# Query, key and value weights loaded one row chunk at a time, and an opening that multiplies the queries chunk by chunk

## The chip, the core and the metric

The kernel runs on one core of one Trainium2 chip. Times are device microseconds of that core. PE is the matmul engine (PEld its weight loads), DVE, ACT and POOL the vector, scalar and GpSimd engines, SP the engine whose queue issues nearly all DMAs.

## The reference, cut to what matters

A layer norm, an attention that carries 8 memory rows from one segment of 32 tokens to the next, a residual sum, and an MLP with its own layer norm. All in bfloat16.

```python
def _A_ref(x, mem0, Wq, Wk, Wv, Wo, seg_len):      # x: 1 x 2048 x 512, H = 32 heads of 128
    ...
    for s in range(n_seg):                          # 64 segments, one after the other
        xs = x[:, s * seg_len:(s + 1) * seg_len, :].copy()
        h = jnp.concatenate([mem, xs], axis=1)      # 8 memory rows + 32 tokens
        q = jnp.einsum('btd,dhe->bhte', h, Wq)
        k = jnp.einsum('btd,dhe->bhte', h, Wk)
        v = jnp.einsum('btd,dhe->bhte', h, Wv)
        scores = jnp.einsum('bhqe,bhke->bhqk', q, k) * scale
        ...
        o = jnp.einsum('bhqk,bhke->bhqe', p, v)
        o = jnp.einsum('bhte,hed->btd', o, Wo)
        mem = o[:, :M, :].copy()                    # what the next segment waits for
        outs.append(o[:, M:, :])
h = x + _A_ref(_layernorm(x, axis=-1), A_mem0, A_Wq, A_Wk, A_Wv, A_Wo, A_seg_len)
h2 = h + _B_ref(_layernorm(h, axis=-1), B_w1, B_b1, B_w2, B_b2)   # gelu(y w1 + b1) w2 + b2, F = 1792
```

Each of Wq, Wk, Wv is 512 x 4096, 4 MB; so is Wo. The 512 rows (`d`) lie on 128 partitions in four chunks of 128 rows (`DC = 4`).

## The kernel before

All weights stay in SBUF: `WQ`, `WK`, `WV` as `[128, 4 chunks, 4096]`, `WO` as `[128, 32, 512]`. A projection of a segment is a pass: for each of the four chunks four matmuls (one for each group of 32 output partitions, side by side on PE), summed in one PSUM bank. A pass gives one half `r` of the 4096 columns. Chunk `c` of half `r` of a weight is a key such as `("WQ", r, c)`; a matmul waits for the DMA that wrote its key.

The 32 tokens of a segment are split. Tokens 0 to 23 with the 8 memory rows are pack A (`hT`); the last 8 tokens of four segments together are pack B (`hB`), a block. `V0`, `K0`, `Q0` and so on are passes of pack A; `("B", "Q", b, (r, bank))` is the pass of pack B of block `b` for the queries' half `r` into a PSUM bank. `SC0`, `SC1` are the scores of each half, `PV0`, `PV1` the products with the values, `SA` the scores of rows without the last 8 tokens, `WO` the output projection in eight units, of which unit `q` reads two pieces of WO.

A recorder (`Sched`) takes every instruction with what it reads and writes; PE's order is written out by hand, and a planner orders the other engines by due times and puts the waits in. For segment 0 the hand-written order is the tuple `START`: strings are parts, `("T", "WO", a, b)` places units `a` to `b - 1` of the projection, `("W", bank, n)` places `n` fill matmuls of 128x512 that nobody reads (function `warm`). A query pass is evacuated by ACT (line 895) or DVE, transposed by DVE in 32x32 blocks (line 917) and copied into `ZC` (lines 931 and 938) for the scores.

SP issues, in this order: four DMAs of 1 MB for each of WV, WK and WQ (line 779), 16 of 256 KB for WO (line 796), then rows of x. The first two tiles of x (`xr`) and two small inputs go through ACT's queue. DVE takes the statistics of both x tiles, then normalizes them; PE's projections start behind that.

Segments 1 to 63 follow `ORDERS`. The memory rows of segment `s` leave as DVE's transpose of the projection (`TT`, line 1191) and a sum into `hT` (line 1185), for which segment `s + 1` waits. `fold` puts the projection of pack B into `opT` on POOL, in pieces of seven instructions; `nat` transposes `opT` back by DMA, adds x, stores `h_mid` and takes the second norm's statistics (`rs2`, on POOL).

The MLP runs in four blocks of 512 rows. Block 0's first matrix product (`w1_first`) is mixed into the end of the attention: six of its 14 column groups are kept as sums and activated later (`gelu_kept`), eight go through PSUM banks 5 and 6 in turn (`early`). `p2_load` fetches rows of `h_mid`, `p2_res` adds the bias row to them on POOL (`hb`, line 1323), the second product (line 1601) sums into four `quad` banks, and DVE adds `hb` to each of these (line 1655) before the next block may write the bank.

Of the kernel before, what the change touches and what calls it, by code (L numbers as in the profile page):

```python
# [104 lines left out]
STEP = 10.28  # L105
OPEN_BANK = dict(K0=4, K1=5, Q0=6, Q1=7, V0=5, V1=4, SC0=6, SC1=7, SA=5, WO=4)
START = (("B", "V", 0, (0, 6), (1, 7)), "V", "X", "S", ("B", "V", 1, (0, 6), (1, 7)), ("B", "K", 0, (0, 4), (1, 6)), "K0", "K1", ("B", "K", 1, (0, 4), (1, 6)),
         ("B", "Q", 0, (0, 5)), "Q0", ("B", "Q", 0, (1, 4)), "Q1", "Z", "SC0", "SC1", ("B", "Q", 1, (0, 5)), "PV0", "PV1", "SA", "WO", ("T", "WO", 0, 3),
         ("T", "WO", 3, 5), ("B", "Q", 1, (1, 6)), ("T", "WO", 5, 6), ("W", 7, 4), ("T", "WO", 6, 7), ("W", 7, 4), ("T", "WO", 7, 8))


def planned(o):
# [456 lines left out]
D = 512  # L569
DC = 4  # L570
# [6 lines left out]
NS = NTOK // SEG  # L577
NTB = NTOK // P
# [48 lines left out]
def build_kernel(nc, A_x, A_mem0, A_Wq, A_Wk, A_Wv, A_Wo, B_w1, B_b1, B_w2, B_b2, out):  # L627
    scale = float(E) ** -0.5
    S = Sched(nc)
    st = contextlib.ExitStack()  # L630
    with st:
# [35 lines left out]
        EC = sb("EC", [P, 2, 2, 64], F32)  # L667
# [3 lines left out]
        SA = sb("SA", [P, 8, 32], F32)  # L671
# [100 lines left out]
        def load(fn, kb, writes):  # L772
            chain.append(S.dma(fn, kb, writes=writes))
        chain, spread = [], {}

        def load_w(W, wd, key):
            for r in range(2):
                for c0 in (0, 2):
                    load(lambda e, r=r, c0=c0: e.dma_start(W[:, c0:c0 + 2, r * 2048:(r + 1) * 2048], wd[:, c0:c0 + 2, r * 2048:(r + 1) * 2048]),  # L779
                         1024, [(key, r, c0), (key, r, c0 + 1)])  # L780

        def first(fn, kb, writes):
            S.dma(fn, kb, writes=writes, eng="act")
# [57 lines left out]
        def warm(bank, n):  # L841

            def f(e):
                for _ in range(n):
                    ins = e.matmul(ps[bank][:, :], ident[:], WV[:, 0, 0:512], start=True, stop=True)
# [474 lines left out]
        def p2_res(k):  # L1320

            for t in range(TBS):
                S.op("pool", lambda e, t=t: e.tensor_tensor(hb[:, k % 2, t, :], hx_of(k)[:, t, :], b2bc[:], ALU.add), reads=[("hx", k % 2), "b2bc"],
                     writes=[("hb", k % 2, t)], after=used["WV"] + S.users([("rs2", NTB - 1)]), dur=1.1)
# [30 lines left out]
        def hx_early(t, after):  # L1355
            S.dma(lambda e: e.dma_start(xT_row, hd[:, t, :]), 128, reads=[("hd", t)], writes=["xT"], after=after)
            S.op("dve", lambda e: e.tensor_scalar(xn[:, t % 2, :], xT_row, agg2[:, t, 0:1], rst2[:, t:t + 1], ALU.subtract, ALU.mult),
                 reads=["xT", ("ag2", t), ("rs2", t)], writes=[("hn0", t), ("xn", t % 2)], dur=0.4)

        def hn_early(t, after):  # L1360
            S.dma(lambda e: e.dma_start_transpose(hnT0[:, :, t, :], xn[:, t % 2, :]), 256, reads=[("xn", t % 2)], writes=[("hnT", "first", t), ("xr", 2 + t)], after=after)

        def gelu_kept(fc):
            g = gT0_home[fc // 2][0][:, fc % 2, :]
            S.op("act", lambda e: e.activation(g, g, ACTF.Gelu_apprx_tanh, bias=b1t[:, fc:fc + 1], scale=1.0),
                 reads=[("gT0", fc), "b1t"], writes=[("gT0", fc)] + gT0_home[fc // 2][1], dur=0.65 + 1.3 * (fc == 0), after=[S.last_writer["SA"], S.last_writer[("EC", 1)]])
# [36 lines left out]
        for s in range(NS):  # L1403
# [48 lines left out]
            def tail(s):  # L1452
                S.tag = (s, "SAT")
                sa_tail(s)
                n = 14 if s == NS - 1 else (4, 4, 6, 0)[s % 4] if s // 4 < NTB - 3 else (7, 7, 0, 0)[s % 4]
                moved = []
                for f in late[::-1]:
                    moved.append(f([S.last_writer[("PTC", 1)]] + [o_ for o_ in moved if o_]))
                late[:] = now
                now.clear()  # L1460
                behind = [S.last_writer[(k, 1)] for k in ("PC", "PCa")] + [o_ for o_ in moved if o_]
                if folds:
                    fold(n, behind + [S.last_writer[("BD", s % 2, j)] for j in range(4 * (s == NS - 1))])
                if turned and s % 4 == 3:
                    for f in turned:
                        f(behind)
                    turned.clear()
                if 0 < s < NS - 1:
                    qb_fill(s + 1, [S.last_writer[("KA", s % 2, 0)]])
                S.tag = None  # L1470
# [55 lines left out]
                    wo(s, bank_of[name], mem=(s + 1 < NS), xrows=(s > 1))  # L1526
            if s == 0:

                for n in START:
                    if n[0] == "B":  # L1530
                        _, what, b, *halves = n
                        for r, bank in halves:
                            if what == "V":
                                v_B(b, r, bank)
                            else:
                                kq_B(b, "KQ".index(what), r, bank)
                    elif n[0] == "T":
                        S.take((0, n[1]), n[2], n[3])
                    elif n == "WO":
                        S.tag = (0, n)  # L1540
                        part(n)
                        S.tag = None
                    elif n[0] == "W":
                        warm(n[1], n[2])
                    elif n == "X":
                        ln1(1)
                    elif n == "S":
                        v_B_turn()
                    elif n == "Z":
# [63 lines left out]
        for i in range(2):  # L1613
            f = slice(i * (F // 2), (i + 1) * (F // 2))
            for c in range(DC):
                S.dma(lambda e, f=f, c=c: e.dma_start(W1[:, c, f], w1_d[:, c, f]), 224, writes=[("W1", i, c)], after=used["WK"])
        p2_load(0)
        p2_norm(1)
        p2_T(1)

# [4 lines left out]
                9: lambda: wo(NS + 1, later[0], mem=False), 11: lambda: nat(NTB - 1)}  # L1625
        rest = dict(zip((0, 1, 2, 3, 4, 5, 7), rest.values()))
        for n, fc in enumerate(range(6, FC)):
            w1_first(fc, early[fc % 2])
            rest.get(n, lambda: None)()
            if n < 6:  # L1630
                gelu_kept(n)
        p2_res(0)
        for fc in range(FC - 4):
            p2_w2(0, fc)
# [79 lines left out]
```

## Time and profile before

| | us |
|---|---|
| median of 3 runs (801.57 to 803.1) | 802.11 |
| the profiled execution | 802.59 |
| its span, from first to last instruction | 800.9 |
| PE busy in the span | 772.0 (96%) |
| DVE, ACT, POOL busy | 616.2, 545.7, 350.9 |

A row of a timeline has its start and length in us, engine, line, operation, `out<-in`, shapes and count, and in brackets how long the engine had been idle and what ended that. A row of the chain of waits has start, length and what the end of the execution hung on at that time. A row of a DMA has how long the issue kept the queue, and below it the time from issue to landing. Ends of matmuls are modelled: a group of N columns side by side shows some 0.2 us more than the step to the next group.

### The profile page before, as it was taken

How to read it: one execution, taken by the hardware profiler on the slowest of the kernel's cores; microseconds unless marked ns; L12 is line 12 of the kernel's file. 1: busy time of each engine (PE TensorE's matmuls, PEld its weight loads, DVE VectorE, ACT ScalarE, POOL GpSimd, SP SyncE). 2: the span in 40 equal slices, each digit the busy share in tenths (PEclk: the TensorE clock that was granted, in tenths of full speed). 3: DMA queues.
4: the chain of work that ended last, by engine and by line, in shares of the span. 5: the costliest groups of instructions: out<-in, count | busy, mean ns of one | idle time of the engine just before them, and what ended most of it. 6: DMA issues, size and time to landing. Idle time of an engine off the chain costs nothing.

```text
span 800.9 us, 43680 instructions
## 1 busy us (share of the span) xinstructions
PE 772.0 (96%) x19403; PEld 417.2 (52%) x18737; DVE 616.2 (77%) x1975; ACT 545.7 (68%) x1622; POOL 350.9 (44%) x886
## 2 busy tenths in 40 slices
PE   3788999999999999999999999999999999999998
PEld 1345555555555555555555555555555555544444
DVE  3267898898989898998989898989898888834211
ACT  1456777777777777777777777777777777743342
POOL 5023334545454545454545454545563535367200
PEclk9999999999999999999999999999999999999999
DMA  8960010110101010101020102020202131275200
GB/s 340 392 191 16 5 27 14 29 32 23 36 18 43 18 43 11 50 7 47 10 51 10 50 10 52 10 51 3 51 23 69 36 80 40 74 169 147 70 27 26
DMA packets 65594, 48.04 MB, mean 60 GB/s; under 512 B 29044, under 2 KB 61820, under 8 KB 65404
## 3 DMA queue, kind: packets, MB, share of 16 engines
q1 hardware_dynamic: 65072, 44.98, 19.3%
q8 instruction: 150, 2.46, 1.3%
q14 instruction: 40, 0.33, 0.1%
q10 hardware_dynamic: 332, 0.27, 0.1%
HBM read 31.08 MB, written 8.13 MB: 49 GB/s over the span
## 4 chain that ended last, share of the span: by engine, by line
PE 90%; DMA 3%; DVE 2%; SPq 2%; POOL 1%; ACT 1%; issue 0%; POOLq 0%
PE ps L876 44%; PE ps L1179 15%; PE ps L609 7%; PE quad L1601 5%; PE ps L1586 4%; PE ps L1218 4%; PE quad L1083 3%; DMA WQ<-in_A_Wq_dram 2%; SPq L779 2%; PE ps L1113 2%; PE quad L1045 2%; PE quad L1151 2%; PE quad L1088 1%; PE ps L1378 1%; PE ps L1375 1%; DMA oN<-opT 1%
## 5 line engine op out<-in xcount | busy, mean ns | idle before, releaser
L876 PE MATMUL ps<-WQ,hT 128*32 128x512 bf16 x2048 | 156.4, 382 | 3.5 <-DVE hT L1185 3.3
L1179 PE MATMUL ps<-WO,OT 128*32 128x256 bf16 x4224 | 140.6, 275 | 0.5 <-ACT OT L894 0.5
L876 PE MATMUL ps<-WV,hT 128*32 128x512 bf16 x1780 | 138.4, 380 | 0.0
L895 ACT ACTIVATE kq<-ps 128x512 bf16<-128x512 f32 x146 | 87.2, 597 | 55.9 <-PE ps L876 55.6
L1134 POOL TENSOR_TENSOR PA<-SA,rsa 128x256 bf16<-128x256 f32 x64 | 39.8, 622 | 184.2 <-DVE rsa L1127 172.3
L894 ACT CAST kq<-ps 128x512 bf16<-128x512 f32 x162 | 94.5, 583 | 29.1 <-PE ps L876 28.3
L1179 PEld LDWEIGHTS ps<-WO,OT 128*32 128x32 bf16 x4224 | 96.3, 97 | 22.1 <-issue 1.7
L1140 POOL COPY BD<-PTA 32x192 bf16<-32x192 bf16 x256 | 96.0, 375 | 16.2 <-DVE PTA L1136 0.4
L1070 DVE SCALAR_TENSOR_TENSOR PC<-EC,rsc,even 128x128 bf16<-128x128 f32 x256 | 94.5, 370 | 6.7
L876 PE MATMUL ps<-WK,hT 128*32 128x512 bf16 x1292 | 91.9, 379 | 0.0
L876 PEld LDWEIGHTS ps<-WQ,hT 128*32 128x32 bf16 x2048 | 55.2, 96 | 68.6 <-issue 20.1
L917 DVE STREAM_TRANSPOSE KALL<-kq 128x256 f32<-128x256 f32 x160 | 70.5, 440 | 19.6 <-ACT kq L894 17.6
L894 ACT CAST VS<-ps 128x512 bf16<-128x512 f32 x189 | 83.9, 444 | 0.9
L1062 ACT ACTIVATE EC<-quad,nmc 128x64 f32<-128x64 f32 x252 | 76.8, 310 | 5.9
L609 PE MATMUL ps<-WK,hT 128*32 128x512 bf16 x756 | 73.8, 379 | 0.0
L894 ACT CAST OT<-quad 128x128 bf16<-128x128 f32 (+1 forms) x207 | 67.8, 349 | 5.7 <-PE quad L1088 0.7
L917 DVE STREAM_TRANSPOSE QT<-kq 128x256 f32<-128x256 f32 x128 | 57.0, 446 | 15.2 <-ACT kq L895 14.1
L876 PEld LDWEIGHTS ps<-WV,hT 128*32 128x32 bf16 x1780 | 48.7, 97 | 37.1 <-issue 2.1
L1589 ACT ACTIVATE WQ<-ps,b1t 128x512 bf16<-128x512 f32 x42 | 28.9, 687 | 53.1 <-PE ps L1586 53.1
L1125 ACT ACTIVATE SA<-SA 128x256 f32<-128x256 f32 x64 | 26.7, 417 | 49.7 <-DVE SA L1124 45.6
L876 PEld LDWEIGHTS ps<-WK,hT 128*32 128x32 bf16 x1292 | 34.9, 97 | 47.8 <-issue 20.4
L1231 POOL TENSOR_TENSOR opT<-TTB,TTS 32x64 bf16<-32x64 f32 x128 | 40.5, 317 | 31.7 <-DVE opT L1185 22.5
(164 smaller groups left out, 1477.1 us busy)
## 6 DMA issues: line engine op xcount, KB each, us to landing
WV<-in_A_Wv_dram SPq DMA_DIRECT2D x4, 1024.0 KB, 10.5
WK<-in_A_Wk_dram SPq DMA_DIRECT2D x4, 1024.0 KB, 17.7
WQ<-in_A_Wq_dram SPq DMA_DIRECT2D x4, 1024.0 KB, 19.2
WO<-in_A_Wo_dram SPq DMA_DIRECT2D x16, 256.0 KB, 7.5
v_last<-VSB SPq DMA_DIRECT2D x60, 64.0 KB, 3.0
VBD<-v_last SPq DMA_DIRECT2D x60, 64.0 KB, 2.9
h_mid<-xr SPq DMA_DIRECT2D x16, 128.0 KB, 1.8
WQ<-h_mid SPq DMA_DIRECT2D x4, 512.0 KB, 4.3
```

Source lines behind the costliest of these rows:

```text
L609: return e.add_instruction(mybir.InstMatmult(name="I-%d" % (4000000 + _kept[0]), engine=mybir.EngineType.PE, start_tensor_calc=start, stop ...
L876: ins = e.matmul(o, l, m, start=(k == 0), stop=(k == DC - 1), tile_position=(0, 32 * j), skip_group_check=True)
L894: return {"act": (lambda e: e.copy(out, src), t_act(n, ps_)), "dve": (lambda e: e.tensor_copy(out, src), 0.155 + 1.0e-3 * n * fast)}
L895: return {"act": (lambda e: e.mul(out, src, scale_), t_act(n, ps_)), "dve": (lambda e: e.tensor_scalar(out, src, scale_, None, ALU.mult), ...
L917: S.op("dve", lambda e: e.transpose(out, src), reads=[("kq", i)], writes=[key], dur=t_dve(256) + 0.02)
L1062: return e.activation(EC[:, r, sl, :], o[:, sl, :], ACTF.Exp, bias=nmc[:, r, sl:sl + 1], accum_out=smc[:, r, sl:sl + 1])
L1070: S.op("dve", lambda e, sl=sl, xc=xc: e.scalar_tensor_tensor(PC[:, r, :, :, sl], xc, rsc[:, r, sl:sl + 1], ev, ALU.mult, ALU.mult), reads= ...
L1134: S.either({k: ((lambda e: e.tensor_tensor(PA[:].rearrange("p a t b -> p a b t"), SA[:].rearrange("p (a b) t -> p a b t", b=2), bc2, ALU.m ...
L1140: S.narrow(S.op("pool", lambda e, j=j, rows=rows: e.tensor_copy(BD[rows, par, :, j, :, :], PTA[rows, :, 0:NA, :]), reads=["PTA"], writes=[ ...
L1179: ins = e.matmul(ps[bank][32 * j:32 * j + 32, 0:256], lhs(slot(h)), wo_cols(h, b), start=(k == 0), stop=(k == 15), tile_position=(0, 32 * ...
L1231: return e.tensor_tensor(o[32 * q:32 * q + 32, c:c + 2], x, y, ALU.add)
L1601: S.op("pe", lambda e, c=c, o=o: e.matmul(o, gT_of(k, fc)[:, t * P:(t + 1) * P], W2[:, fc, c], start=(fc == 0), stop=(fc == FC - 1)), read ...
```

## The change

It has five parts. The three weights are loaded by chunk: one DMA brings 128 whole rows of 8192 B, where one DMA brought half of the columns of two chunks, in pieces of 4096 B. In segment 0 the four query passes that stood one after the other are cut into their chunks (`("D", name, part)` records a part and takes its PE instructions out of the order, `("G", name, a, b)` puts pieces `a` to `b - 1` back): chunk 0 of all four, chunk 1 of all four, and so on, with fill matmuls between. At the hand-over to the MLP the banks of `w1_first` are swapped, the kept activations are grouped differently, and block 0's `hb` no longer waits for the last statistics, with its load issued before W1 instead of behind it. In the last blocks a fold is cut into two or three with waits of their own, and the first early norm waits for segment 54's memory rows.

```diff
         def load_w(W, wd, key):
-            for r in range(2):
-                for c0 in (0, 2):
-                    load(lambda e, r=r, c0=c0: e.dma_start(W[:, c0:c0 + 2, r * 2048:(r + 1) * 2048], wd[:, c0:c0 + 2, r * 2048:(r + 1) * 2048]),
-                         1024, [(key, r, c0), (key, r, c0 + 1)])
+            for c in range(DC):
+                load(lambda e, c=c: e.dma_start(W[:, c, :], wd[:, c, :]), 1024, [(key, 0, c), (key, 1, c)])
 ...
-         ("B", "Q", 0, (0, 5)), "Q0", ("B", "Q", 0, (1, 4)), "Q1", "Z", "SC0", "SC1", ("B", "Q", 1, (0, 5)), "PV0", "PV1", "SA", "WO", ("T", "WO", 0, 3),
+         ("D", "B0", ("B", "Q", 0, (0, 5))), ("D", "A0", "Q0"), ("D", "B1", ("B", "Q", 0, (1, 4))), ("D", "A1", "Q1"),
+         ("G", "B0", 0, 1), ("G", "A0", 0, 1), ("G", "B1", 0, 1), ("G", "A1", 0, 1), ("G", "B0", 1, 2), ("G", "A0", 1, 2), ("G", "B1", 1, 2), ("G", "A1", 1, 2), ("W", 3, 5),
 ...
-                     writes=[("hb", k % 2, t)], after=used["WV"] + S.users([("rs2", NTB - 1)]), dur=1.1)
+                     writes=[("hb", k % 2, t)], after=used["WV"] + ([S.last_writer[("opB", (NTB - 1) % 2)]] if k == 0 else []), dur=1.1)
 ...
                 if folds:
+                    if 4 < s < NS - 1 and (n == 7 or s % 4 == 0):
+                        fold(1, behind[:2])
+                        fold(3, behind)
+                        n -= 4
+                        behind = behind + [S.last_writer[("hTm", (s + 1) % RING)]]
                     fold(n, behind + [S.last_writer[("BD", s % 2, j)] for j in range(4 * (s == NS - 1))])
 ...
+                    if n[0] == "D":
+                        m = len(S.pe_order)
+                        opening(n[2])
+                        pieces[n[1]] = S.pe_order[m:]
+                        del S.pe_order[m:]
+                    elif n[0] == "G":
+                        S.pe_order.extend(pieces[n[1]][n[2]:n[3]])
 ...
-        p2_load(0)
+            if i == 0:
+                p2_load(0)
 ...
-            w1_first(fc, early[fc % 2])
+            w1_first(fc, early[(fc + 1) % 2])
             rest.get(n, lambda: None)()
-            if n < 6:
-                gelu_kept(n)
+            if n == 0:
+                gelu_kept(0)
+                gelu_kept(1)
+            if n == 5:
+                for i in range(2, 6):
+                    gelu_kept(i, [S.last_writer[("gT0", fc - 1)]])
```

Three places of the order show it. The first is PE in the opening, from the last key pass to the values (`hB` is pack B, `hT` pack A; `KALL,ZC` are the scores). Before:

```order
L876 MATMUL ps<-WK,hB 32x512 x32
L876 MATMUL ps<-WQ,hB 32x512 x16
L876 MATMUL ps<-WQ,hT 32x512 x16
L876 MATMUL ps<-WQ,hB 32x512 x16
L876 MATMUL ps<-WQ,hT 32x512 x16
L1045 MATMUL ps<-KALL,ZC 32x64 x32
L876 MATMUL ps<-WQ,hB 32x512 x16
L1083 MATMUL quad<-PTC,VS 128x2x16 x8
```

The same place now, from the fills behind chunk 1 (`WV,ident` are fills) to the scores:

```order
L847 MATMUL quad<-WV,ident 128x512 x5
L878 MATMUL ps<-WQ,hB 32x512 x4
L878 MATMUL ps<-WQ,hT 32x512 x4
L878 MATMUL ps<-WQ,hB 32x512 x4
L878 MATMUL ps<-WQ,hT 32x512 x4
L847 MATMUL quad<-WV,ident 128x512 x5
L878 MATMUL ps<-WQ,hB 32x512 x4
L613 MATMUL ps<-WQ,hB 32x512 x4
L878 MATMUL ps<-WQ,hT 32x512 x4
L613 MATMUL ps<-WQ,hT 32x512 x4
L878 MATMUL ps<-WQ,hB 32x512 x16
L1047 MATMUL ps<-KALL,ZC 32x64 x32
```

Passes of 16 became rounds of four groups of four, and the query pass of block 1 moved ahead of the scores. Behind the scores there are now fills too (five, then two between the values' halves), and the eight fills between the last units of WO became six.

The second is PE at the end of segment 63 (numbers are PSUM banks; `xr,QTB` is `w1_first`, `KALL,QT` the scores `SA`). Before:

```order
L1113 MATMUL ps5<-KALL,QT 32x32 x32
L1218 MATMUL ps4<-WO,OTB 32x512 x12
L1378 MATMUL ps5<-xr,QTB 128x512 x4
L1179 MATMUL ps7<-WO,OT 32x256 x64
L1378 MATMUL ps6<-xr,QTB 128x512 x4
```

Now:

```order
L1115 MATMUL ps5<-KALL,QT 32x32 x32
L1220 MATMUL ps4<-WO,OTB 32x512 x12
L1380 MATMUL ps6<-xr,QTB 128x512 x4
L1181 MATMUL ps7<-WO,OT 32x256 x64
L1380 MATMUL ps5<-xr,QTB 128x512 x4
```

The first of the two groups left the bank that holds the scores `SA`.

The third is POOL at the end of the attention (`opT` closes a fold, `rst` are the second norm's statistics, `WV<-WQ,b2bc` is `hb`). Before:

```order
L1233 COPY TTS<-TTB 64x256
L1234 TENSOR_TENSOR TTB<-TTB,TTS 64x256
L1235 COPY TTS<-TTB 32x256
L1231 TENSOR_TENSOR opT<-TTB,TTS 32x8x8 x4
L1262 TENSOR_SCALAR rst<-agg 128x1
L1263 TENSOR_TENSOR rst<-rst,cneg 128x1
L1262 TENSOR_SCALAR rst<-agg 128x1
L1263 TENSOR_TENSOR rst<-rst,cneg 128x1
L1323 TENSOR_TENSOR WV<-WQ,b2bc 128x512 x16
```

Now:

```order
L1235 COPY TTS<-TTB 64x256
L1236 TENSOR_TENSOR TTB<-TTB,TTS 64x256
L1237 COPY TTS<-TTB 32x256
L1233 TENSOR_TENSOR opT<-TTB,TTS 32x8x8 x4
L1325 TENSOR_TENSOR WV<-WQ,b2bc 128x512 x7
L1264 TENSOR_SCALAR rst<-agg 128x1
L1265 TENSOR_TENSOR rst<-rst,cneg 128x1
L1325 TENSOR_TENSOR WV<-WQ,b2bc 128x512 x2
```

Seven sums `hb` moved ahead of the statistics; one more stands earlier, between segments 62 and 63.

More of the change, by code (lines that the diff above doesn't have):

```diff
@@ L107 @@
 START = (("B", "V", 0, (0, 6), (1, 7)), "V", "X", "S", ("B", "V", 1, (0, 6), (1, 7)), ("B", "K", 0, (0, 4), (1, 6)), "K0", "K1", ("B", "K", 1, (0, 4), (1, 6)),
-         ("B", "Q", 0, (0, 5)), "Q0", ("B", "Q", 0, (1, 4)), "Q1", "Z", "SC0", "SC1", ("B", "Q", 1, (0, 5)), "PV0", "PV1", "SA", "WO", ("T", "WO", 0, 3),
-         ("T", "WO", 3, 5), ("B", "Q", 1, (1, 6)), ("T", "WO", 5, 6), ("W", 7, 4), ("T", "WO", 6, 7), ("W", 7, 4), ("T", "WO", 7, 8))
[6 rows of a table added]
 def planned(o):
@@ L844, in f @@
                 for _ in range(n):
-                    ins = e.matmul(ps[bank][:, :], ident[:], WV[:, 0, 0:512], start=True, stop=True)
+                    ins = e.matmul(quad[:, bank, :], ident[:], WV[:, 0, 0:512], start=True, stop=True)
                 return ins
@@ L1357, in hx_early, with gelu_kept @@
             S.op("dve", lambda e: e.tensor_scalar(xn[:, t % 2, :], xT_row, agg2[:, t, 0:1], rst2[:, t:t + 1], ALU.subtract, ALU.mult),
-                 reads=["xT", ("ag2", t), ("rs2", t)], writes=[("hn0", t), ("xn", t % 2)], dur=0.4)
+                 reads=["xT", ("ag2", t), ("rs2", t)], writes=[("hn0", t), ("xn", t % 2)], dur=0.4, after=[S.last_writer[("hTm", 54 % RING)]] if t == 0 else ())
         def hn_early(t, after):
             S.dma(lambda e: e.dma_start_transpose(hnT0[:, :, t, :], xn[:, t % 2, :]), 256, reads=[("xn", t % 2)], writes=[("hnT", "first", t), ("xr", 2 + t)], after=after)
-        def gelu_kept(fc):
+        def gelu_kept(fc, after=()):
             g = gT0_home[fc // 2][0][:, fc % 2, :]
             S.op("act", lambda e: e.activation(g, g, ACTF.Gelu_apprx_tanh, bias=b1t[:, fc:fc + 1], scale=1.0),
-                 reads=[("gT0", fc), "b1t"], writes=[("gT0", fc)] + gT0_home[fc // 2][1], dur=0.65 + 1.3 * (fc == 0), after=[S.last_writer["SA"], S.last_writer[("EC", 1)]])
+                 reads=[("gT0", fc), "b1t"], writes=[("gT0", fc)] + gT0_home[fc // 2][1], dur=0.65 + 1.3 * (fc == 0), after=[S.last_writer["SA"], S.last_writer[("EC", 1)], *after])
         def w1_first(fc, bank, keep=False):
@@ L1527, in build_kernel, with opening @@
             if s == 0:
-                for n in START:
-                    if n[0] == "B":
+                pieces = {}
+                def opening(n):
+                    if n[0] == "D":
[5 more added lines that the diff above has]
+                        S.pe_order.extend(pieces[n[1]][n[2]:n[3]])
+                    elif n[0] == "B":
                         _, what, b, *halves = n
@@ L1553, in build_kernel @@
                         part(n)
+                for n in START:
+                    opening(n)
                 tail(0)
```

4 rows, old and new, of the table START are left out of this document.

## The prediction

> **What bounds the kernel now.** I read the page first, then a table of stretches, then the chain that ended last, then the opening and the hand-over to the MLP instruction by instruction.
>
> ```profile
> span 800.9 us, 43680 instructions
> 0.00:51.56 51.56, 30.70 (x482) 13.91 (x474) 17.48 (x43) 18.00 (x44) 12.42 (x51) 0.93 0.97 353
> 100.00:690.00 590.00, 589.82 (x16794) 326.13 (x15982) 525.53 (x1728) 448.39 (x1393) 284.89 (x729) 1.00 0.13 32
> 690.00:710.00 20.00, 19.64 (x457) 11.01 (x442) 13.29 (x37) 15.13 (x34) 10.52 (x27) 1.00 0.48 144
> 710.00:740.00 30.00, 29.06 (x137) 12.64 (x134) 10.90 (x19) 8.24 (x12) 20.41 (x30) 1.00 0.62 154
> ```
>
> A row of a stretch has its length, then busy time (and count) of PE, PE's weight loads, DVE, ACT and POOL, the granted clock, the DMA share and GB/s. PE sets the time. From 100 to 690 us it idles 0.18 us of 590, so an edit there can hardly gain; POOL has half of that stretch free (284.89 busy). What can be won is idle PE in the opening (51.56 - 30.70 = 20.9 us) and small holes in 690 to 740 (0.36 + 0.94). In the opening the DMA engines are full (share 0.97). The chain there:
>
> ```profile
> 17.92 18.75 DMA WQ<-in_A_Wq_dram
> 36.72 2.76 PE ps L876 x24
> 39.50 0.61 ACT kq L895
> 40.13 0.46 DVE QT L917
> 40.60 0.31 ACT ZC L931
> 40.95 0.34 PE ps L1045 x13
> 44.40 2.17 PE ps L1179 x40
> 50.59 0.46 DVE TT L1191
> ```
>
> The last piece of WQ lands at 17.92 + 18.75 = 36.67. Then come the rest of the queries, their evacuation, the scores, the output projection (L1179) from 44.40, and at 50.59 the transpose that leads to segment 1. But a second limit runs beside that chain, the landing of WO:
>
> ```profile
> L796 SPq DMA_DIRECT2D WO<-in_A_Wo_dram x2: 668/686/704, 40.9 to 41.7; - x2
> DMA to landing us min/median/max: 6.9/7.0/7.0
> 47.86 1.04 PE L845 MATMUL ps<-WV,ident 128*128 128x512 bf16 x4
> 50.13 0.40 PE L1179 MATMUL ps<-WO,OT 128*32 128x256 bf16 x8
> ```
>
> The last WO piece lands at 41.7 + 6.9 = 48.6, and the unit that reads it runs at 50.13: compute is 1.5 us behind its data. Part of that is the granted clock, 0.50 in two stretches of 3.4 us, the first of which follows one where PE was busy for 0.67 us of 3.41; the projection starts in the second:
>
> ```profile
> 33.36:36.77 3.41, 0.67 (x12) 0.18 (x16) 0.45 (x1) 0.92 (x3) 0.00 (x0) 1.00 1.04 373
> 36.78:40.18 3.40, 3.01 (x40) 0.97 (x40) 0.50 (x2) 1.25 (x3) 0.74 (x2) 0.50 1.10 348
> 43.61:47.00 3.39, 3.34 (x90) 2.77 (x94) 1.79 (x5) 1.11 (x4) 0.00 (x0) 0.50 1.10 350
> ```
>
> **The change part by part.** *Weights by row chunks.* Twelve DMAs of 1 MB stay twelve and keep their place on SP; each partition now gets one row of 8192 B where it got two of 4096 B. 3072 row packets become 1536. Prices, from two stretches of the weight queue (10 to 11 us: 4096 B rows only; 38 to 44 us: 1024 B rows) and one 8 KB packet of another queue (11 to 13 us):
>
> ```profile
> DMA packets 100, 0.41 MB, mean 410 GB/s; under 512 B 0, under 2 KB 0, under 8 KB 100
> DMA packets 2168, 2.09 MB, mean 348 GB/s; under 512 B 127, under 2 KB 2168, under 8 KB 2168
> q14 instruction: 1, 0.01, 1.0%
> ```
>
> At 410 GB/s one of 16 engines needs 16 x 4096 / 410 = 159.8 ns a row; at 348 GB/s, 47.1 ns for 1024 B. The line through both is 9.5 ns a packet plus 0.0367 ns a byte. Leaving out 1536 packets saves 1536 x 9.5 / 16 = 0.9 us (estimate): the last WQ chunk lands at 35.8, the last WO piece, behind it in the queue, at 47.7. From both sides: the 8 KB packet took 1.0% of 16 x 2 us = 320 ns, by rounding 304 to 336, against 319.6 for two rows. That is from 96 x 15.6 ns = 1.5 us gained to 96 x 16.4 ns = 1.6 us lost. I take 0.9: the line rests on thousands of packets and lies inside.
>
> The Trainium skill ("DMA: Bandwidth & Descriptors", section "Where 436 GB/s comes from") says that a transfer from HBM to SBUF is held by the HBM side at about 358 GB/s a core. By that rule longer rows would bring nothing and the sum would lack this 0.9; the trace disagrees, with 410 GB/s.
>
> A pass over one half of the columns now needs all four chunks of its weight, where it needed two DMAs:
>
> ```profile
> L779 SPq DMA_DIRECT2D WV<-in_A_Wv_dram x1: 862/862/862, 2.3 to 2.3; - x1
> DMA to landing us min/median/max: 13.5/13.5/13.5
> L779 SPq DMA_DIRECT2D WK<-in_A_Wk_dram x1: 2343/2343/2343, 7.0 to 7.0; - x1
> DMA to landing us min/median/max: 19.0/19.0/19.0
> 14.72 3.60 PE L876 MATMUL ps<-WV,hB 128*32 128x512 bf16 x32 [0.35 <-ACT hB L894]
> 25.58 1.90 PE L876 MATMUL ps<-WK,hB 128*32 128x512 bf16 x32
> 29.05 1.91 PE L876 MATMUL ps<-WK,hB 128*32 128x512 bf16 x32
> 30.78 0.60 PE L876 MATMUL ps<-WQ,hB 128*32 128x512 bf16 x8
> ```
>
> WV's fourth lands at 15.8; its matmuls are due 12/32 into the 3.60 us from 14.72, at 16.1. WK's lands at 26.0, due at 25.58 + 12/32 x 1.73 = 26.2. Both are just in time even without faster DMA: 0, at worst 0.2 us, which the fills below absorb.
>
> *Queries by chunk.* Four chunk rounds of 16 matmuls (1.73 / 2 = 0.87 us each) start at 30.78, with five fill matmuls (0.97 / 4 each, so 1.2 us) after the second and third: 30.78 + 3 x 0.87 + 2 x 1.2 = 35.8, just when the last chunk lands. PE is then nearly full from 33.4 to 36.8, where it had 0.67 us, so I expect full clock. The last round ends at 36.7; before, 2.76 us of PE followed the landing. The cost: four query evacuations (0.6 us) now come at once where two had been done at 32 to 34 us. ACT does three and DVE one, then four transposes of 0.46 on DVE: 36.1 + 0.6 + 4 x 0.46 = 38.5, ZC 0.31, second scores at 38.9 instead of 40.95. Scores to projection took 44.40 - 40.95 = 3.45, so it starts at about 42.4; five units, the query pass, three units and two fills of three at full clock add 1.2 + 0.87 + 0.72 + 1.5, so compute is ready for the last unit at about 46.4. The last WO piece (47.7) is now late by 1.3 us, and PE waits for it. The opening ends 50.13 - 47.7 = 2.4 us earlier: 0.9 from the DMA, 1.5 from compute that no longer lags.
>
> The fills after the scores (five and two, 1.7 us) lie in the 3.45 us in which the chain there runs over DVE and ACT; 0. Changed instruction counts of segment 0 shift only the weight loads that pad segment 1; 0 by the count.
>
> *Hand-over to the MLP.*
>
> ```profile
> 697.24 0.84 PE L1218 MATMUL ps<-WO,OTB 128*32 128x512 bf16 x12
> 698.45 1.04 PE L1378 MATMUL ps<-xr,QTB 128*128 128x512 bf16 x4 [0.36 <-DVE SA L1124]
> 714.77 1.48 POOL L1231 TENSOR_TENSOR opT<-TTB,TTS 32x64 bf16<-32x64 f32 x4
> 724.93 11.25 POOL L1323 TENSOR_TENSOR WV<-WQ,b2bc 128x512 f32<-128x512 bf16 x10
> 729.09 0.39 PE L1601 MATMUL quad<-WK,WQ 128*128 128x512 bf16 x1 [0.22 <-DVE WV L1655]
> 730.20 0.39 PE L1601 MATMUL quad<-WK,WQ 128*128 128x512 bf16 x1 [0.72 <-DVE WV L1655]
> 728.27 0.59 PE L1601 MATMUL quad<-WK,WQ 128*128 128x512 bf16 x2
> ```
>
> The first L1378 group waits for DVE to leave bank 5. With the banks swapped it starts on bank 6, 12 x 0.054 = 0.65 us after 697.24: 698.45 - 697.89 = 0.56 gained (0.36 by the idle time alone). The four L1601 of 728.27 end at 730.42 (730.20 + 0.22) instead of 728.27 + 4 x 0.216 = 729.13, since the residual sums on POOL start only at 724.93. Now they stand behind the last opT sums, which end at 716.25; four of 1.12 us are done by 720.8, before the quad banks fill. Gain 1.29 (0.94 by idle time alone). The statistics that go behind them on POOL are read by the last block's norms some 30 us later. One sum now stands between the last two segments on POOL, ahead of the last segment's softmax product; POOL is busy 10.52 of 20 us there, so 0, at worst its 1.12. The residual's load goes ahead of four W1 pieces and five transposing DMAs on SP: 0, since these are read only when block 1 begins, behind the eight L1601 groups; at worst its one issue, some 0.4. The regrouped GELUs leave PE free while ACT has 20 - 15.13 us idle there: 0, at worst one activation of 0.7. The split folds and the later first norm: 0, with no idle PE to win and POOL half empty.
>
> **Sum.** 0.9 + 1.5 + 0.56 + 1.29 = 4.25. The profiled execution took 802.59 (span 800.9 and 1.7 around it) and would take 798.3; it stands 0.48 above the median 802.11, so the median becomes 797.9.
>
> **Rivals.**
>
> *Rows of 8 KB are no faster (0.18).* Then the opening ends by WO at 48.6, and 1.5 + 1.85 = 3.35 us remain: 798.8. At the bad end (1.6 lost) 800.4. For it: the one 8 KB packet at 320 ns; against: 348 against 410 GB/s by row size.
>
> *The second x tile comes late (0.16); the case on the other side.*
>
> ```profile
> 2.25 0.47 ACTq L770 DMA_DIRECT2D xr<-in_A_x_dram  x1
> 10.46 0.69 DVE L810 BATCH_NORM_STATS2 stt<-xr 128x6 f32<-128x512 bf16 x1 [4.57 <-DMA xr<-in_A_x_dram]
> ```
>
> All PE work of the opening hangs on this tile: DVE serves it before the first normalized tile, and PE starts 4.26 us behind it (14.72). Its small rows share the engines with the weights; it took 8.2 us for 128 KB. If it waits for a number of rows, rows of twice the length can delay it by up to 8.2. Compute has 1.3 us in hand, so the sum is used up at a delay of 1.3 + 4.25 = 5.6 us, and from 7.2 on the kernel is slower by over 0.2%; at 8.2, 802.11 + 2.6 = 804.7 (chance 0.06). At 3 to 5 us, 799.6 to 801.6 (0.10). Against: if it waits for a number of bytes or whole transfers, nothing changes. The Trainium skill ("DMA: Bandwidth & Descriptors", section "Queues, rings and completion order") says that each engine takes its queues in turn, a whole packet at a time. That speaks for this rival; no row here shows how the turns go with 8 KB rows.
>
> *The hand-over's waits come back elsewhere (0.08):* the wait moves to an activation or a W1 piece; 2.4 remain: 799.7.
>
> **How the numbers follow.** Forecast 0.58, rivals 0.18, 0.16, 0.08. A measurement of this kernel can tell about 0.2%, 1.6 us: faster means under 800.5. The forecast, the third rival and nearly all of the first lie there: 0.80; within 0.2%: 0.13; slower: 0.07. The range goes from 797.0 (1.5 from the DMA and a little more) to 801.0, taking in the first and third rivals and part of the second; the likeliest case alone has 797.0 to 799.0.
>
> **What would show it.** Right: WQ's last landing near 35.8 and WO's near 47.7; the weight queue near 420 GB/s; the last projection unit of the opening waiting for the DMA; TT near 48.2; full clock from 33 to 48 us; no DVE wait at the first L1380 group or in the second block's first sums. Wrong: bn_stats of the second x tile well after 10.5, scores after 41, the clock at half at the projection, or a new PE wait at 695 to 735.

## The result, and the profile after

| | before | after |
|---|---|---|
| median of 6 runs, us | 802.76 (801.57 to 803.69) | 797.76 (796.75 to 798.64) |
| ratio, 95% interval | | 0.9938 (0.9926 to 0.9951) |
| span of the profiled execution, us | 800.9 | 795.5 |

The change made the kernel 5.0 us faster, 0.6%. The same stretches of the profiled execution of after, the first one ending again where segment 1 begins (48.65 us instead of 51.56); columns as before:

```profile
0.00:48.65 48.65, 30.91 (x493) 13.54 (x481) 17.95 (x44) 17.14 (x43) 12.50 (x51) 1.00 0.99 372
100.00:690.00 590.00, 589.77 (x16784) 333.61 (x15961) 524.87 (x1733) 451.10 (x1398) 287.53 (x735) 1.00 0.13 33
690.00:710.00 20.00, 19.95 (x379) 11.05 (x373) 12.24 (x31) 13.57 (x26) 12.21 (x30) 1.00 0.69 190
710.00:740.00 30.00, 29.89 (x138) 13.28 (x139) 9.24 (x19) 9.05 (x14) 16.23 (x21) 1.00 0.53 131
```

PE is busy as long as before in an opening that is 2.9 us shorter; from 18.2 us on, where its record begins, the clock is full; the holes of 690 to 740 are nearly closed (0.05 + 0.11 idle, before 0.36 + 0.94). The chain of waits of the opening now ends in the DMA, not in compute:

```profile
40.01 7.18 DMA WO<-in_A_Wo_dram
47.23 0.43 PE ps L1181 x8
47.69 0.46 DVE TT L1193
```

Where the 5.4 us of the spans went is read from four points that both traces have: how much earlier each stands after the change.

| point | before | after | gained so far | in this piece |
|---|---|---|---|---|
| TT of segment 0 | 50.59 | 47.69 | 2.90 | 2.90 opening |
| TT of segment 63 | 697.03 | 693.39 | 3.64 | 0.74 segments |
| first product behind segment 63 | 698.45 | 694.38 | 4.07 | 0.43 banks |
| first product of block 1 behind its four first sums | 730.42 | 725.04 | 5.38 | 1.31 residual sums |

The rows of after for the last two, PE's timeline, with the group of the second product (L1619) ahead of the last:

```profile
694.38 1.04 PE L1380 MATMUL ps<-xr,QTB 128*128 128x512 bf16 x4
724.17 1.03 PE L1619 MATMUL quad<-WK,WQ 128*128 128x512 bf16 x4
725.04 1.03 PE L1604 MATMUL ps<-WQ,WK 128*128 128x512 bf16 x4
```

None carries a bracket any more: PE waits for nothing there.

The landings. The first row of each pair is one DMA's issue, the second its time to landing. Before, the first DMA of WV; then after, the first of WV, the last of WQ and the last of WO:

```profile
L779 SPq DMA_DIRECT2D WV<-in_A_Wv_dram x1: 451/451/451, 0.8 to 0.8; - x1
DMA to landing us min/median/max: 6.7/6.7/6.7
```

```profile
L782 SPq DMA_DIRECT2D WV<-in_A_Wv_dram x1: 393/393/393, 0.8 to 0.8; - x1
DMA to landing us min/median/max: 5.4/5.4/5.4
L782 SPq DMA_DIRECT2D WQ<-in_A_Wq_dram x1: 2214/2214/2214, 7.5 to 7.5; - x1
DMA to landing us min/median/max: 27.7/27.7/27.7
L798 SPq DMA_DIRECT2D WO<-in_A_Wo_dram x1: 668/668/668, 40.0 to 40.0; - x1
DMA to landing us min/median/max: 7.2/7.2/7.2
```

The first MB lands at 6.2 us where it landed at 7.5; WQ ends at 35.2 (before 36.67) and WO at 47.2 (before 48.6). Nearly all of the lead of 1.4 us is there after the first MB, but before cut that MB from other places too (half rows of two chunks), so row length need not be all of it; the run with half rows, below, tells the two apart. In a stretch just behind the start (3 to 5 us), and in one well behind it (20 to 30 us), before:

```profile
q1 hardware_dynamic: 129, 0.53, 84.8%
DMA packets 1054, 4.07 MB, mean 407 GB/s; under 512 B 63, under 2 KB 63, under 8 KB 1053
```

and after:

```profile
q1 hardware_dynamic: 91, 0.75, 89.3%
DMA packets 574, 4.19 MB, mean 419 GB/s; under 512 B 64, under 2 KB 64, under 8 KB 64
```

From 3 to 5 us a row of 4096 B took 0.848 x 16 x 2 us / 129 = 210 ns of an engine, a row of 8192 B 0.893 x 32 / 91 = 314 ns: 0.53 against 0.75 MB. Later the two differ by 3%, 407 to 419 GB/s.

### The profile page after: what moved, and what is told of

The parts are those of the page before. It is cut to its first block, busy times and chain, and to the rows that moved or that the text cites. A ratio compares the mean times of both kernels' runs of the same rounds, so it can differ in the third digit from the quotient of the medians.

```text
span 795.5 us, 43693 instructions
## 1 busy us (share of the span) xinstructions
PE 770.5 (97%) x19407; PEld 424.5 (53%) x18723; DVE 614.6 (77%) x1976; ACT 546.6 (69%) x1621; POOL 351.1 (44%) x886
## 4 chain that ended last, share of the span: by engine, by line
PE 92%; SPq 5%; DVE 1%; DMA 1%; issue 0%; ACT 0%
PE ps L878 44%; PE ps L1181 15%; PE ps L613 7%; PE quad L1619 6%; PE ps L1604 5%; PE ps L1220 4%; SPq L798 4%; PE quad L1085 3%; PE quad L1047 2%; PE ps L1115 2%; PE quad L1153 2%; SPq L782 1%; PE quad L1090 1%; PE ps L1380 1%; DMA WO<-in_A_Wo_dram 1%; PE ps L1377 1%
## 5 line engine op out<-in xcount | busy, mean ns | idle before, releaser
L878 PE MATMUL ps<-WQ,hT 128*32 128x512 bf16 x2044 | 158.4, 380 | 3.9 <-DVE hT L1187 3.3
L878 PE MATMUL ps<-WK,hT 128*32 128x512 bf16 x1292 | 93.7, 379 | 0.0
L878 PEld LDWEIGHTS ps<-WQ,hT 128*32 128x32 bf16 x2044 | 57.5, 96 | 65.3 <-issue 18.6
L613 PE MATMUL ps<-WK,hT 128*32 128x512 bf16 x756 | 75.8, 379 | 0.0
L878 PEld LDWEIGHTS ps<-WV,hT 128*32 128x32 bf16 x1780 | 52.3, 97 | 34.0 <-issue 1.7
L878 PEld LDWEIGHTS ps<-WK,hT 128*32 128x32 bf16 x1292 | 36.7, 97 | 46.5 <-issue 19.2
L1233 POOL TENSOR_TENSOR opT<-TTB,TTS 32x64 bf16<-32x64 f32 x128 | 40.1, 314 | 34.4 <-DVE opT L1187 22.5
```

The costliest lines, as they stand in the source:

```text
L613: return e.add_instruction(mybir.InstMatmult(name="I-%d" % (4000000 + _kept[0]), engine=mybir.EngineType.PE, start_tensor_calc=start, stop ...
L878: ins = e.matmul(o, l, m, start=(k == 0), stop=(k == DC - 1), tile_position=(0, 32 * j), skip_group_check=True)
L1233: return e.tensor_tensor(o[32 * q:32 * q + 32, c:c + 2], x, y, ALU.add)
```

## The experiments

Each was timed beside the kernel before, except the three that say one look. Ratios are to the kernel before on the same chip.

| | median us | ratio (95%) | TT of segment 0 | span |
|---|---|---|---|---|
| after, first comparison | 797.76 | 0.9938 (0.9926 to 0.9951) | 47.69 | 795.5 |
| half rows throughout | 800.07 | 0.9961 (0.9948 to 0.9974) | 49.15 | 796.1 |
| loads alone | 802.32 | 0.9984 (0.9974 to 0.9994) | 49.53 | 799.6 |
| fold split alone | 802.09 | 0.9985 (0.9976 to 0.9995) | 51.09 | 800.9 |
| hand-over alone | 801.20 | 0.9975 (0.9964 to 0.9986) | 50.36 | 798.8 |
| after, again | 797.85 | 0.9932 (0.9917 to 0.9946) | 47.58 | 795.8 |
| without fills | 798.15 | 0.9937 (0.9920 to 0.9954) | 47.67 | 797.8 |
| without fold split | 798.53 | 0.9940 (0.9925 to 0.9954) | 47.65 | 798.1 |
| statistics later | 797.50 | 0.9930 (0.9916 to 0.9944) | 47.70 | 795.3 |
| half rows in WV (one look) | 800.43 | | 49.64 | 798.5 |
| half rows in WK, WQ (one look) | 799.74 | | 48.53 | 797.8 |
| without fills, again (one look) | 798.87 | | 47.60 | 797.0 |
| copies later | 797.26 | 0.9930 (0.9917 to 0.9944) | 47.54 | 795.1 |

**Row length.** The changed kernel with each chunk in two DMAs:

```diff
             for c in range(DC):
-                load(lambda e, c=c: e.dma_start(W[:, c, :], wd[:, c, :]), 1024, [(key, 0, c), (key, 1, c)])
+                for r in range(2):
+                    load(lambda e, c=c, r=r: e.dma_start(W[:, c, r * 2048:(r + 1) * 2048], wd[:, c, r * 2048:(r + 1) * 2048]), 512, [(key, r, c)])
```

> The changed kernel, with each weight chunk loaded by two DMAs of 512 KB whose rows are 4096 B, instead of one of 1 MB with rows of 8192 B. Chunk order, opening and hand-over stay. Theory S (long rows help mainly while the DMA engines start up): the first WV chunk lands at about 7.5 us instead of 6.2, the last WO piece at 48.6 instead of 47.2, TT of segment 0 at 49.1 instead of 47.7, time 797.8 + 1.4 = 799.2. Theory P (9.5 ns a packet, evenly, as in the prediction): last WO piece at 48.1, time 798.7, and the first chunk less than 0.1 us later. Theory N (row length is nothing, the order of the chunks is all): 797.8.

The last unit of the opening, and its TT:

```profile
48.70 0.40 PE L1182 MATMUL ps<-WO,OT 128*32 128x256 bf16 x8 [0.26 <-DMA WO<-in_A_Wo_dram]
49.15 0.45 DVE L1194 STREAM_TRANSPOSE TT<-ps 128x256 f32<-128x256 f32 x1 [2.53 <-PE ps L1182]
```

WO lands at 41.5 + 7.2 = 48.7 and PE waits for it: 1.46 us behind the changed kernel. That is S's size; N has fallen. The first chunk missed S: its second half lands at 6.7, where S said 7.5 and P less than 6.3. So 0.5 of the 1.46 is there after the first chunk, and about 1 when WV is in (15.4; in the traces with rows of 8192 B 14.2 to 14.6). The time moved by 1.8 (0.9961 against 0.9938), in another comparison; the intervals allow S and P.

Then half rows in WV alone, and in WK and WQ alone (one look each):

> The changed kernel with half rows (4096 B, two DMAs of 512 KB a chunk) in WV alone; WK and WQ keep rows of 8192 B. Read from the landings, not from the time. Theory S (short rows cost most while the DMA engines start up and the small rows of x go beside them): most of the 1.46 us of the run with half rows throughout comes back: last WO piece at 48.2 or later, TT of segment 0 at 48.7 or later. Theory P (9.5 ns a packet everywhere): a third of 0.9, WO at 47.5, TT at 48.0.

> The changed kernel with half rows in WK and WQ, and rows of 8192 B in WV. Theory S: the first chunks land as in the changed kernel (6.2 us for the first), last WO piece at 47.6 at most, TT at 48.1 at most. Theory P: two thirds of 0.9 later, WO at 47.8, TT at 48.3.

The last WO piece of the first, and of the second:

```profile
L800 SPq DMA_DIRECT2D WO<-in_A_Wo_dram x1: 663/663/663, 41.1 to 41.1; - x1
DMA to landing us min/median/max: 7.0/7.0/7.0
```

```profile
L800 SPq DMA_DIRECT2D WO<-in_A_Wo_dram x1: 666/666/666, 41.0 to 41.0; - x1
DMA to landing us min/median/max: 7.1/7.1/7.1
```

48.1 in both, 0.9 behind the changed kernel. A third of the rows costs 0.9, three times P's price; but the other two thirds cost 0.9 as well, where S gave 0.4 at most and P 0.6. Neither theory holds alone: short rows cost more at the start than later, and more than 9.5 ns later too. The two parts add to 1.8 where both together cost 1.46; each is one look, and how it splits stays open. TT in the first (49.64) is 1.5 later than its landing; there the clock was half from 26.5 to 29.9 us, which would put compute behind, but nothing was run to show that.

**Loads alone.** The kernel before with the new `load_w` and nothing else.

> The kernel before, with the three weights loaded by row chunks of 8192 B and nothing else changed: the query passes stand one after the other as before and there are no new fills. Theory S: WQ's last landing at 35.2 and WO's at 47.2 as in the changed kernel, but the four query passes all wait for the last chunk, so some 2.8 us of PE follow it, the clock falls to half as before, and the projection still ends behind WO: TT near 49.1 instead of 50.6, time 802.8 - 1.5 = 801.3. Prediction's split (0.9 from the DMA): 801.9. Rival (the opening's gain is all from the loads): TT near 47.7, 799.9.

Its WO lands at 40.1 + 7.0 = 47.1, as in the changed kernel. Its chain of waits:

```profile
7.55 27.59 DMA WQ<-in_A_Wq_dram
35.18 4.54 PE ps L874 x39
49.03 0.48 PE ps L1177 x8
```

Behind the last chunk come 4.54 us of query passes, partly at half clock (0.50 from 34.9 to 38.3), and the last unit starts 1.9 us behind its data. TT gains 1.06 of the changed kernel's 2.90: the landing came 1.4 earlier, compute did not follow. S has the landing right and TT 0.4 too early (49.53 for 49.1); the rival's 47.7 has fallen. The other 1.84 belongs to the new opening, and by the run without fills, next, to its order.

**Fills.** The changed kernel without its fill matmuls, timed, and looked at a second time. All `("W", 3, n)` are taken out of `START`: 5 + 5 + 5 + 2 + 3 + 3 = 23, not the 21 of the expectation.

> The changed kernel without the 21 fill matmuls of its opening. Theory C (the fills keep the clock full, and that is what lets compute catch up with WO): the granted clock falls to half in one or two stretches of 3.4 us between 30 and 50 us, the projection's units and the last query pass there take twice as long, compute is ready for the last unit 1 to 2 us behind the last WO piece at 47.2, TT at 48.5 to 49.2: 0.8 to 1.5 slower than the changed kernel. Rival D (the landings bind alone): TT stays at 47.7, the time the same.

> The kernel without the fill matmuls a second time, for one look at where its clock falls. In its first trace TT of segment 0 came at 47.7 as with the fills, and segment 1 took 1.7 us longer at half clock (49.5 to 52.9). Theory C2 (after idle PE in 34 to 47 us a half stretch falls into segment 1): segment 1 is 1 to 2 us longer again. Rival (the half stretch fell there by chance): TT of segment 1 follows that of segment 0 by 10.2 as with the fills.

In the first, the last unit of the opening, and four stretches with their clock (the column behind the five engines). The clock changes here only at steps of 3.41 us, counted from where its record begins (18.75 us in this trace), and the stretches are cut at these steps:

```profile
47.21 0.40 PE L1180 MATMUL ps<-WO,OT 128*32 128x256 bf16 x8 [0.86 <-DMA WO<-in_A_Wo_dram]
```

```profile
39.23:42.64 3.41, 1.40 (x76) 1.19 (x79) 2.73 (x12) 2.66 (x12) 0.00 (x0) 1.00 1.10 348
42.64:46.06 3.42, 3.42 (x56) 2.06 (x48) 1.15 (x4) 0.83 (x2) 0.00 (x0) 0.50 1.10 351
46.06:49.47 3.41, 1.53 (x32) 0.75 (x60) 2.13 (x7) 0.18 (x1) 0.62 (x1) 1.00 0.75 224
49.47:52.88 3.41, 3.41 (x37) 1.62 (x73) 1.72 (x6) 1.18 (x2) 2.08 (x7) 0.50 0.35 96
```

The clock falls as theory C says, in the middle of the projection, and still the last unit waits 0.86 us for WO: D is right for the end of segment 0, where compute had the slack. The price comes one step later: a second half stretch lies in segment 1, where every step hangs on the one before. TT of segment 1, first without fills, then with them (TT of segment 0 stands in the table):

```profile
59.52 0.45 DVE L1192 STREAM_TRANSPOSE TT<-ps 128x256 f32<-128x256 f32 x1 [0.37 <-PE ps L1180]
```

```profile
57.85 0.45 DVE L1193 STREAM_TRANSPOSE TT<-ps 128x256 f32<-128x256 f32 x1 [0.36 <-PE ps L1181]
```

Segment 1 takes 11.85 us without fills (11.86 in the second look), 10.16 with them, as C2 says. But the fills alone do not decide it. The run with half rows in WK and WQ, above, has all of them, and its segment 1 took 11.87 us at half clock all the same (49.59 to 53.01). Its TT of segment 1 and the stretch ahead of that half stretch; then the stretch of the changed kernel that lies there:

```profile
60.40 0.45 DVE L1195 STREAM_TRANSPOSE TT<-ps 128x256 f32<-128x256 f32 x1 [0.38 <-PE ps L1183]
46.18:49.59 3.41, 1.78 (x24) 0.58 (x39) 1.25 (x5) 0.00 (x0) 0.10 (x1) 1.00 0.89 264
```

```profile
45.51:48.92 3.41, 1.83 (x27) 0.68 (x47) 1.16 (x4) 0.00 (x0) 0.28 (x1) 1.00 0.87 271
```

PE was busy for 1.83 us there and the clock stayed full; the 1.78 us of the other run were too few. The fills raise this busy time from about 1.5 us to just enough, 1.83 in the first trace of the changed kernel and 1.94 in the repeat, so the margin is narrow. Over the executions they do help: the mean granted clock on record was 1.000 in all 11 of the changed kernel (6 and 5); without fills it was 1.000 in one of six, 0.998 in one and 0.995 or 0.996 in four, which took 796.91 to 800.42 us. In the timed comparison the difference of the medians (0.3 us) is too small to tell from none.

**The folds.** The kernel before with the fold split alone, and the changed kernel without it:

```diff
                 if folds:
+                    if 4 < s < NS - 1 and (n == 7 or s % 4 == 0):
+                        fold(1, behind[:2])
+                        fold(3, behind)
+                        n -= 4
+                        behind = behind + [S.last_writer[("hTm", (s + 1) % RING)]]
```

> The kernel before, with the fold split alone (first piece behind the first PC, three behind both, the rest behind the next memory rows). Theory F (a sum opT on POOL that runs beside the sum hT on DVE makes that 0.16 us longer, on the chain between two segments): the longer segments behind 8, 12, 16, 28, 36, 40, 48, 56 and 61 lose 0.15 each, some of it lost again at 48, 52 and 56: 802.8 - 0.7 = 802.1, at most 1.4 less. Prediction's rating of this part (0): 802.8.

> The changed kernel with the fold in one piece as before. Theory F (sums on POOL beside the sum hT on DVE): the sum hT is 0.16 longer again in the segments after 8, 12, 16, 28, 36, 40, 48, 53, 56, 61, and the memory rows of segment 63 come 1.1 later against those of segment 0: 0.7 to 1.1 slower than the changed kernel. Prediction's rating: the same.

The condition cuts the first fold of every block from segment 8 on in two, and both folds of the last blocks in three; it is not a matter of the last blocks alone.

The sum `hT` on DVE that brings the memory rows into the next segment, all 126 halves of it (shortest/median/longest in ns), in before, after, fold split alone, and without fold split:

```profile
L1185 DVE TENSOR_TENSOR hT<-TT x126: 186/189/357, 51.1 to 687.5; 64x32 bf16<-64x32 f32 x126
```

```profile
L1187 DVE TENSOR_TENSOR hT<-TT x126: 185/189/191, 48.2 to 683.9; 64x32 bf16<-64x32 f32 x126
```

```profile
L1185 DVE TENSOR_TENSOR hT<-TT x126: 186/189/190, 51.6 to 686.9; 64x32 bf16<-64x32 f32 x126
```

```profile
L1187 DVE TENSOR_TENSOR hT<-TT x126: 185/189/356, 48.1 to 686.3; 64x32 bf16<-64x32 f32 x126
```

What stands beside a long one, at segment 8 of before, DVE's row and then POOL's; and the same place of after:

```profile
132.78 0.55 DVE L1185 TENSOR_TENSOR hT<-TT 64x32 bf16<-64x32 f32 x2
132.77 0.31 POOL L1231 TENSOR_TENSOR opT<-TTB,TTS 32x64 bf16<-32x64 f32 x1
```

```profile
129.92 0.39 DVE L1187 TENSOR_TENSOR hT<-TT 64x32 bf16<-64x32 f32 x2
129.46 0.32 POOL L1233 TENSOR_TENSOR opT<-TTB,TTS 32x64 bf16<-32x64 f32 x1
```

Where POOL's sum starts first, by 0.01 us, DVE's takes 0.16 longer, on the chain between two segments. With the fold in pieces POOL's sum is over before DVE's begins, and the next waits behind it. Worked out over all segments: in each of the four traces with the fold in one piece 17 of the sums `hT` are over 0.02 us longer than the median (0.74 to 1.76 us in sum, according to which engine came first), in each of the ten with the split none. From TT of segment 1 to that of segment 63 the four take 636.27, 636.04, 636.14 and 638.01 us, the ten 634.68 to 636.13, with means of 636.6 and 635.5. The two groups overlap, and the last of the four has a stall of its own (below); without it the means are 0.8 apart. The medians move by 0.7 us when the split is taken out (within the intervals) and by 1.3 when it is put in, although the opening of that trace was 0.5 late, at half clock from 37.9 to 48.1 us. Theory F holds: the longer sums and what removes them are shown, and they are worth about 1 us by these means. The 638.01 has one stall of 1.4 us that F does not explain: in segment 55 DVE waited, in its order, for the row of the early norm, and the queries' transposes behind it were late.

```profile
616.65 0.41 DVE L1359 TENSOR_SCALAR xn<-xT,agg,rst 128x512 bf16<-128x512 bf16 x1 [1.64 <-DMA xT<-h_mid]
```

The Trainium skill ("SBUF — State Buffer", section "Who interferes with whom") says that a DVE instruction with two inputs in SBUF contends with a GpSimd instruction that reads SBUF, that the ports they share are an exclusive lock, and that issue order decides who blocks. The traces agree on who waits, not on how long: 0.16 us, where waiting for the whole of POOL's sum would have been 0.30.

**Hand-over.** The kernel before with the bank swap, the regrouped activations, the freed residual sums and their earlier load.

> The kernel before, with the edits of the hand-over alone (banks of the first product swapped, activations regrouped, the residual sums freed from the last statistics, their load issued earlier). Theory H (the prediction's two terms, as the two traces have them): 0.43 from the banks and 1.3 from the residual sums, 802.8 - 1.75 = 801.0. Rival (the residual sums are early only because everything ahead of them is): the banks alone, 802.3.

The first product behind segment 63; in block 1, the four first sums (L1601) and the product behind them:

```profile
697.66 1.04 PE L1378 MATMUL ps<-xr,QTB 128*128 128x512 bf16 x4
727.46 1.03 PE L1601 MATMUL quad<-WK,WQ 128*128 128x512 bf16 x4
728.32 1.03 PE L1586 MATMUL ps<-WQ,WK 128*128 128x512 bf16 x4
```

TT of segment 63 is 0.36 earlier than in before, the first product 698.45 - 697.66 = 0.79, and block 1's product behind the four sums 730.42 - 728.32 = 2.10: 0.43 from the banks and 1.31 from the sums. Theory H holds, and the parts do not depend on the opening. Which edit does what is read from where the time is gained; the regrouped activations and the earlier load were not taken apart from the rest, nor was the later first norm ever run alone.

**The same kernel again, and two more waits.**

> The changed kernel itself, once more, so that the three runs beside it have a measure on the same chip, and for one question: in its first trace the heads of segments 48, 52 and 56 lose 0.2 us each, because the weight loads of the first pass come two first and the rest 0.21 us behind. Theory I (it belongs to the program's place in the instruction stream): the same three heads lose the same again. Theory E (it belongs to the execution, since the run with half rows has the same steady program and none of it): other heads or none. Time 797.8, 5.0 less than before.

The loads of the first pass at the head of segment 48, first trace, then the repeat:

```profile
529.68 0.09 PEld L878 LDWEIGHTS ps<-WQ,hT 128*32 128x32 bf16 x1
529.92 0.53 PEld L878 LDWEIGHTS ps<-WQ,hT 128*32 128x32 bf16 x8
```

```profile
530.74 0.34 PEld L878 LDWEIGHTS ps<-WQ,hT 128*32 128x32 bf16 x8
```

None of the three heads loses it again, but the repeat loses 0.1 to 0.3 us in eleven others, only three of which (27, 35 and 43) the first trace has too: theory E. What splits these loads is not settled. Some of the repeat's other losses have a cause. In segments 27, 35, 39 and 43 TT starts 0.56 to 0.62 us behind the last projection matmul instead of 0.33, and at 27 DVE's rows before it are long beside a copy on POOL (DVE's row, then POOL's):

```profile
322.57 0.86 DVE L1187 TENSOR_TENSOR opT<-TT 64x96 bf16<-64x96 f32 x2
322.78 0.53 POOL L836 COPY hT<-xT 128x384 bf16<-128x384 bf16 x1
```

Two edits to the changed kernel went for this: the first half of the second norm's statistics, which stands on DVE behind these rows, was put behind the next memory rows, or the copies on POOL were. The second edit:

```diff
                     for f in turned:
-                        f(behind)
+                        f(behind + [S.last_writer[("hTm", (s + 1) % RING)]])
```

> The changed kernel with one more edit: in the folds of blocks 4, 6 and 8 the first half of the second norm's statistics (DVE, 0.43 us) goes behind the next memory rows, where DVE waits 0.37 for an evacuation, instead of just ahead of the transpose TT that closes segments 27, 35 and 43. Theory: TT there starts 0.33 us behind the last projection matmul as elsewhere instead of 0.48, and the three segments lose 0.15 each: 0.45 faster than the changed kernel, seen in the trace rather than in the time. Rival: the transpose of the queries behind it is late by 0.06 and hands that on to the scores: 0.3 faster.

> The changed kernel with one more wait: the two copies on POOL that bring a new block's transposed rows into hB and hT (xT in segments 7, 11, 15 and so on) start behind the next memory rows instead of behind the last PC. The blocks they serve are read several segments later. Theory F2 (the same collision of POOL and DVE in another place: beside these copies DVE's sum opT takes 0.74 to 0.86 for its two halves instead of 0.52, or the sum xr 0.63 instead of 0.43, and TT behind them is 0.1 to 0.3 late at segments 27, 35, 39 and 43): TT starts 0.33 behind the last projection matmul in every segment, 0.45 to 0.9 faster than the changed kernel's 797.8, with segment 1's TT to segment 63's at 635.0 or less. Rival (DVE is late there for another reason, or the copies collide behind the memory rows instead): 635.5 to 636.0 as in the two traces of the changed kernel.

With the statistics moved, TT is on time at 27, 35 and 43, and at 39, which was not moved, it is 0.15 late. With the copies moved it is on time (0.33) in every segment, and the same sums at 27 take what they take alone:

```profile
322.75 0.53 DVE L1187 TENSOR_TENSOR opT<-TT 64x96 bf16<-64x96 f32 x2
```

So what makes TT late is shown: DVE's sums beside the copies, with the statistics still to come ahead of TT. A gain is not: segments 1 to 63 take 635.29 us, between the two traces of the changed kernel (635.53, 636.00) and F2's 635.0, since heads of other segments lost time. 797.26 is the lowest median of all, and its interval covers that of the changed kernel: not shown to be faster.

## Why the prediction was right, and where it was not

The time (797.76 for 797.9) and the gain (ratio 0.9938, where 797.9 / 802.11 = 0.9947) came out as forecast, but two terms were too small. That the time hit to 0.14 us is luck in part: the gain was 5.0 us where the sum has 4.25, and the kernel before measured 802.76 where the forecast started from 802.11.

| term | predicted | measured |
|---|---|---|
| DMA of the opening | 0.9 | 1.4 |
| compute no longer behind WO | 1.5 | 1.5 |
| bank swap | 0.56 | 0.43 |
| residual sums earlier | 1.29 | 1.31 |
| folds (all of segments 1 to 63) | 0 | 0.7 |
| sum | 4.25 | 5.4 |

*DMA.* The line of 9.5 ns a packet gave 35.8 and 47.7 for the last landings; they came at 35.2 and 47.2. The step that failed is the pair of stretches it was drawn through, 10 to 11 and 38 to 44 us: both lie behind the start, and by the run with half rows about 1 of the 1.46 us that short rows cost is there when WV is in, at 15 us. The rate behind the start, about 420 GB/s, was right (419).

*Compute.* In before the last unit ran 1.5 us behind its data, now 0.04, and it waits for the DMA as forecast. The second scores came at 38.3 (38.9 forecast), the projection at 42.2 (42.4), TT at 47.69 (48.2). The clock was full from 18.2 us to the end of the opening.

But the reason given, that the fills keep the clock and so let compute catch up, was only half right. The order by chunks does it: at half clock without fills the last unit still waited for WO. What the fills protect is segment 1, 1.7 us, which the prediction did not count; and in the changed kernel that was a near thing: 1.83 us of busy PE ahead of it, where 1.78 failed in another run.

*Hand-over.* Both terms held, alone and with the rest; the banks gave what the idle time said (0.36) rather than the step count (0.56).

*Folds.* Costed at 0 "with no idle PE to win and POOL half empty". That is the step that was wrong in kind. A PE busy by the record is not a PE that cannot be late: segments 1 to 63 became 0.74 us shorter, yet PE's idle time from 100 to 690 us was 0.18 before and 0.23 after. Matmul ends are modelled, so such gaps need not show. The loss sat on DVE between the last projection and the next segment's first pass. POOL's busy share said nothing about where its sums fell.

*Rivals.* Rows of 8 KB were faster. The second x tile came earlier than in before (10.46), not later:

```profile
9.85 0.69 DVE L812 BATCH_NORM_STATS2 stt<-xr 128x6 f32<-128x512 bf16 x1 [3.11 <-DMA xr<-in_A_x_dram]
```

No wait came back between 690 and 740 us.

## What to carry to other kernels

When a stretch is bound by landings, cut the work into the pieces that land, so that only one piece's work is left behind the last one. Filler for the clock then counts for the stretch after it, where one step hangs on the next; read its margin from PE's busy time between two steps of the clock. In a chain of short steps look at each small operation's longest duration beside its median: where they differ, find what runs on the neighbouring engine at that moment, and move that by a wait, however idle that engine is. Price a DMA's row length from a stretch of the same phase, the start apart from the steady flow.

## What the runs showed that was not expected

- Short rows are dearest at the start: 4096 B took 210 ns of an engine at 3 to 5 us and 159.8 at 10 to 11; 8192 B took 314 at the start.
- An add of 0.19 us on DVE became 0.35 beside a sum on POOL that began 0.01 us before it; a pair of 0.53 became 0.86 beside a copy.
- Half clock followed stretches in which PE was far from idle. In the first 120 us of the 13 traces that record the clock there, it fell from full to half twelve times; in the 3.41 us ahead of each fall PE was busy for 0.40 to 1.78 us. Behind 1.78 it also stayed full once (at 32.0 us in the second look without fills), and behind 1.83 or more every time. PE's busy time is modelled, so the border is rough. The Trainium skill ("TensorE: Matmul & The Clock Gate", section "Part 1: The HAM clock gate") ties the fall to an idle window of about 3.4 us; the traces agree on the length, but the window need not be idle.
- Beside a packet of 16 KB of the instruction queue, which holds one DMA engine for 1.1 us, one landing step of the weights is 0.1 to 1.2 us longer than its neighbours in each trace. In the changed kernel the packet starts at 24.5 us, and from WK's last chunk to WQ's first it takes 3.1 us instead of 2.5; in the run with half rows in WV the step takes 3.7, so its 0.9 may not be row length alone. That the packet is the cause is not shown.
- Executions of one program differ by 0.5 us between segments 1 and 63 (635.53 and 636.00), in which segments lose 0.1 to 0.3 us each.
